# A fused retention and MLP kernel on one TensorE: first units reordered, part one's running sums on ScalarE and GpSimd, x^T copied in halves

## The chip, the core and the metric

The kernel runs on one core of one Trainium2 chip. A core has a matrix engine (TensorE, "PE" in the profile, with its weight loads as "PEld"), three engines for elementwise work (VectorE "DVE", ScalarE "ACT", GpSimd "POOL") and SyncE ("SP"), which here only issues transfers. The engines run side by side; each takes its own instructions in the order in which the program lists them, and semaphores hold an instruction back until its inputs are there. TensorE writes into accumulation banks (PSUM), from which VectorE or ScalarE copy the results into the core's memory.

The metric is the device time of one execution in microseconds (us).

## What is computed

```python
# q, k, v: (8, 8, 576, 64)  batch, heads, sequence, head size; float32
scores = scale * q @ k^T                       # per batch and head
ret = scores * Dmat                            # Dmat[i, j] = gamma[h] ** (i - j) for i >= j, else 0
attn = ret @ v
x = attn.transpose(0, 2, 1, 3).reshape(4608, 512)
h = x @ w_in                                   # w_in (512, 2048)
g = max(h, 0) + alpha * min(h, 0)              # alpha (2048,)
out = g @ w_out                                # w_out (2048, 512)
```

## The kernel before

**Retention in chunks.** The sequence of 576 rows is cut into nine chunks of 64. Within a chunk the scores are multiplied by a triangular mask; what earlier chunks contribute goes through a state of 64 x 64 per head, the running sum of k^T v over the chunks before. Powers of gamma are folded into q and v beforehand (`part_scale`, `scale_pair`).

**The MLP in units.** The 4608 rows of x are cut into 18 blocks of 256 (`kb`). The 2048 hidden columns are cut into eight groups (`i`) of two times 128. A *unit* is one (block, group): a first product (x^T with a slice of `w_in` into the bank `ph`), the activation on the engines beside TensorE (into `g`), and a second product (`g` with a slice of `w_out`, added up over the eight groups in the banks `po`). Blocks 2 to 17 use a form with seven instead of eight products and combined weights (`mlp_unit`, L450). Blocks 0 and 1, whose weights are only just arriving, use the plain form: `plain_unit` (L411), `plain_relu` (L430), `plain_out` (L391).

**Weights come in pieces.** Each group has four pieces: two for `w_in`, two for `w_out`, fetched as raw float64 words and turned into float32 on three engines. `piece_in` (L286) puts two ScalarE instructions into the program (L297, L299). `piece_out` (L302) puts in three on VectorE (L308, L311, L313) and one addition on GpSimd (L315), and then issues the next fetch. Pieces 0 and 1 are the first group's `w_in`, 2 and 3 its `w_out`, 4 and 5 the second group's `w_in`, 6 and 7 its `w_out`.

**The first batch in parts.** The retention of batch 0, from which blocks 0 and 1 are made, is computed ahead in three *parts* of 4, 4 and 1 chunks, all eight heads at once. The steps of a part `x`:

- `part_scale(x, i)` (L615): GpSimd multiplies q (`i` = 1) or v (`i` = 2) by its powers of gamma, two halves, L621.
- `part_transposes(x, i)` (L633): TensorE turns k or q, four tiles at a time, L641; copies at L648 (one of part zero's at L646).
- `part_scores(x)` (L650): TensorE L660, 64 instructions in the trace; mask at L667 (VectorE) for the first part, and at L669, L670 (copy on ScalarE, mask on GpSimd) for the second.
- `part_states(x)` (L672): TensorE L680, then the running sums: `sums[x][0..3]`. For the first part L688 copies on ScalarE the first bank slice, and L690 adds on VectorE one slice at a time.
- `part_values(x)` (L697): TensorE L706 with the masked scores, then L717 with the running sums; chunk `j` uses `sums[x][j - 1]`. Even chunks go into bank 0, odd ones into bank 1. Then x^T is copied out: L722 copies bank 0 (128 partitions x 512 elements), L724 copies bank 1 in two halves of 64 partitions.
- `part_carry(x)` (L693): GpSimd makes the start of the next part from the last sum, L694.

In the names "part one" of the change is part 0 of the code, and "q's part two" is q of part 1.

**Order.** Up to L881 the order of every engine's instructions is the order in which the program lists them (a manual schedule). L766 to L828 list the beginning by hand: parts, pieces and the units (0,0), (0,1), (1,0), (1,1) in turn. Then a loop (L864) does the other twelve plain units with the retention of two head pairs of batch 1 in the gaps, and after that the main loop runs the other blocks. A unit's second product is listed one unit after its first product.

**Loads.** SyncE issues nearly all loads in program order. In the beginning `load` (L78) holds a load back until the one that lies `IN_FLIGHT` = 5 x 256 KB of loads ahead of it has landed.

Of the kernel before, what the change touches and what calls it, by code (L numbers as in the profile page):

```python
# [14 lines left out]
ALU = mybir.AluOpType  # L15
# [3 lines left out]
def kernel(  # L19
# [10 lines left out]
    nc = tc.nc  # L30
# [5 lines left out]
    NPAIR = H // 2  # L36
# [32 lines left out]
    def half(x):  # L69
        return slice(x * C, (x + 1) * C)  # L70
# [1 line left out]

    IN_FLIGHT = 5 << 18
    flight = []

    def load(to, src, size):  # L78
        ins = nc.sync.dma_start(to, src)
        if gated[0]:  # L80
            ahead = size
            for other, n in reversed(flight):
                if ahead >= IN_FLIGHT:
                    tc.add_manual_dep(ins.ins, other.ins.name, mybir.DependencyInfo(
                        mybir.DependencyClass.Sync, mybir.DependencyReason.DATA),
                        reason="bytes in flight")
                    break
                ahead += n
            flight.append((ins, size))

    gated = [True]

# [59 lines left out]
    def load_part(x):  # L154
        j0, j1 = PARTS[x]
        for i, src in ((0, k), (1, q), (2, v)):
            for m in range((j1 - j0 + 1) // 2):
                s0 = (j0 + 2 * m) * C
                rows = min(P, j1 * C - s0)
                to, fro = part[x][i][0:rows, m], src[0, :, s0:s0 + rows].rearrange("h p d -> p h d")  # L160
                if x == 0 and i == 1:
                    nc.scalar.dma_start(to, fro)
                else:
                    load(to, fro, rows * DM * 4)
# [29 lines left out]
    for i in range(NBIT - 1):  # L194
# [8 lines left out]
                            op=ALU.mult)  # L203
# [61 lines left out]
    def fetch(n):  # L265
        while npiece[0] < min(n, len(pieces)):
            srcs, at = pieces[npiece[0]][0], npiece[0]
            npiece[0] += 1
            free[:] = [t for t in free if at < gone.get(t, len(pieces))]
            t = free.pop(0)  # L270
            if isinstance(t, str):
                raw = ring.tile([P, 4 * HM], INT32, tag=t, name=f"raw_{at}")
            else:
                raw = w_in[t][:, 4:6].rearrange("p s u c f -> p (s u c f)").bitcast(INT32)
            for i, src in enumerate(srcs):
                to = raw
                if len(srcs) > 1:
                    to = raw.rearrange("p (x e f two) -> p x e f two", x=2, e=2, two=2)[:, :, i]
                load(to, src, P * 4 * HM * 4 // len(srcs))
            raws.append((raw, t))  # L280
# [90 lines left out]
            t0 = kb * TB + m * P  # L371
            nc.sync.dma_start(out[t0:t0 + P, :], osb[:, m].rearrange("p x f -> p (x f)"))

    def mlp_out():
        kb, i, g = pend.pop(0)
        if kb in PLAIN:
            return plain_out(kb, i, g)
        if i == 0:
            acc[kb] = [ps_o.tile([P, 2, HM], FP32, tag=f"pso{n}", name=f"po{n}_{kb}")
                       for n in range(4)]  # L380
        for n, (x, y) in enumerate(PROD):
            nc.tensor.matmul(acc[kb][n // 2][:, n % 2, :], g[:, x, :], w_out[i][:, y, :],  # L382
                             start=(i == 0 and n % 2 == 0),
                             stop=(i == NU - 1 and (n % 2 == 1 or n == 6)),
                             skip_group_check=True)
        if i == NU - 1:
            out_block(kb, acc.pop(kb))

    def plain_out(kb, i, g):  # L391
        if i == 0:
            acc[kb] = [ps_o.tile([P, DM], FP32, tag=f"pso{2 * kb + m}", name=f"po{m}_{kb}")
                       for m in range(2)]
        for m in range(2):
            for x in range(2):
                nc.tensor.matmul(acc[kb][m], g[:, 2 * x + m],  # L397
                                 w_out[i][:, 2 * x:2 * x + 2].rearrange("p x f -> p (x f)"),
                                 start=(i == 0 and x == 0), stop=(i == NU - 1 and x == 1))
        if i == NU - 1:  # L400
            po = acc.pop(kb)
            osb = ring.tile([P, 2, DM], FP32, tag=f"o{kb}", name=f"osb_{kb}")
            for m in range(2):
                t0 = kb * TB + m * P
                nc.scalar.copy(osb[:, m], po[m])
                nc.sync.dma_start(out[t0:t0 + P, :], osb[:, m])
        if kb == PLAIN[-1] and i % UST == UST - 1:
            waiting.extend((w_in[i // UST], x) for x in S_WORK)
            waiting.extend((w_out[j], x) for j in range(i + 1 - UST, i + 1) for x in T_WORK)
# [262 lines left out]
    def part_states(x):  # L672
        kn, vn = part[x][0], part[x][2]
        banks = [t.rearrange("p (m c d) -> p m c d", m=2, c=NPAIR)
                 for t in part_banks(x, None if x == 0 else 0, "pu")]
        for m in range(2):
            for c in range(NPAIR):
                for p2 in range(2):
                    for h2 in range(2):
                        nc.tensor.matmul(banks[p2][half(h2), m, c], kn[half(p2), m, 2 * c + h2],  # L680
                                         vn[half(p2), m, 2 * c + h2],
                                         start=(m == 0 and c == 0),
                                         stop=(m == 1 and c == NPAIR - 1), skip_group_check=True)
        was = carry[x]
        for j in range(4):
            u = banks[j % 2][:, j // 2]
            if was is None:
                nc.scalar.copy(sums[x][j], u)  # L688
            else:
                nc.vector.tensor_tensor(out=sums[x][j], in0=was, in1=u, op=ALU.add)  # L690
            was = sums[x][j]
# [5 lines left out]
    def part_values(x):  # L697
        vn, qT, at = part[x][2], tT[x, 1], tat[x]
        banks = [t.rearrange("p (c m s) -> p c m s", c=NPAIR, m=2)
                 for t in part_banks(x, 0 if x == 0 else None, "pv")]  # L700
        for m in range(2):
            for c in range(NPAIR):
                for p2 in range(2):
                    for h2 in range(2):
                        n = 2 * c + m
                        nc.tensor.matmul(banks[p2][half(h2 ^ p2), c, m],  # L706
                                         vn[half(p2), m, 2 * c + h2],
                                         at[half(p2), h2, n * C:(n + 1) * C],
                                         start=(m == 0 and c == 0), stop=False,
                                         skip_group_check=True)  # L710
        for j in range(1 if x == 0 else 0, 4):
            su = sums[x][j - 1] if j else carry[x]
            for c in range(NPAIR):
                for h2 in range(2):
                    for e in range(0, D, 32):
                        to = (h2 ^ (j % 2)) * D + e
                        nc.tensor.matmul(banks[j % 2][to:to + 32, c, j // 2],  # L717
                                         su[half(h2), c, e:e + 32], qT[half(h2), c, chunk(j)],
                                         start=False, stop=(j >= 2), skip_group_check=True)
        xb[x] = ring.tile([P, NCC, TB], FP32, tag=f"x{x}", name=f"xb_{x}")  # L720
        to = xb[x].rearrange("p c (m q s) -> p q c m s", m=2, q=2)
        nc.scalar.copy(to[:, 0], banks[0])  # L722
        for h2 in range(2):
            nc.scalar.copy(to[half(h2), 1], banks[1][half(1 - h2)])  # L724


    def last_transposes():
# [37 lines left out]

    fetch(6)  # L766
    load_part(1)
    fetch(8)
    load_part(2)
    part_scale(0, 1)  # L770
# [1 line left out]
    part_transposes(0, 1)  # L772
    part_scale(0, 2)
    part_scores(0)
    part_states(0)
    piece_in(2)
    piece_out(2)
    part_carry(0)
    part_values(0)
    aps = ps_a.tile([P, NFC], FP32, tag="psa", name="aps")  # L780
    nc.tensor.transpose(aps, a16, ident[0:NFC, 0:NFC])
    nc.vector.tensor_copy(alpha, aps)
    nc.vector.tensor_scalar(nalpha, alpha, -1.0, None, ALU.mult)
    piece_in(3)
    piece_out(2)
    part_scale(1, 1)
    piece_in(1)
    plain_unit(0, 0)
    plain_relu()
    piece_out(1)  # L790
    part_scale(1, 2)
    part_transposes(1, 0)
    mlp_out()
    part_transposes(1, 1)
    piece_out(1)
    piece_in(1)
    piece_out(1)
    part_scores(1)
    part_states(1)
    part_scale(2, 1)  # L800
    part_scale(2, 2)
    piece_in(1)
    plain_unit(0, 1)
    piece_out(1)
    plain_relu()
    piece_in(1)
    part_values(1)
    part_carry(1)
    last_transposes()
    mlp_out()  # L810
# [14 lines left out]
    piece_in(1)  # L825
    piece_out(1)

    gated[0] = False  # L828

# [108 lines left out]
```

## Time and profile before

| | |
|---|---|
| median of the four runs | 1027.4 us (1026.47, 1027.32, 1027.48, 1028.34) |
| time of the profiled execution | 1027.32 us |
| its span, first to last instruction | 1025.6 us |
| TensorE: busy, share of the span | 1008.2 us, 98% |
| VectorE | 770.0 us, 75% |
| ScalarE | 267.4 us, 26% |
| GpSimd | 176.9 us, 17% |
| TensorE clock granted, mean | 0.996 |
| bytes moved | 64.30 MB, mean 63 GB/s |

The profiled execution is one of the four runs, 0.08 us from their median; 1.7 us of its time lie outside its span. TensorE's share is 6 tenths in the first of 40 slices (of 25.6 us each) and 9 tenths or more in all others but the last (8), and the granted clock is 8 tenths in the first slice and 9 or more after it. From 43.4 us on TensorE runs without a gap. Most of what the change touches lies in the first 45 us, so the table of the whole says little about it; that stretch is read from its timeline, its waits and its chain.

### The profile page before, as it was taken

The page shows a single profiled execution, that of the slowest core. Times are in us where ns is not written, and L with a number is a line of the kernel's source. Part 1 is how long each engine was busy: PE and PEld are TensorE (multiplying, and loading weights), DVE is VectorE, ACT ScalarE, POOL GpSimd, SP SyncE. Part 2 cuts the span into 40 slices and gives each one's busy share as a digit, 9 for nine tenths or more (in the row PEclk, how much of TensorE's full clock was granted, in tenths as well). Part 3 has the DMA queues.
Part 4 walks back from the last instruction along what each step waited for, and adds up shares of the span by engine and source line. Part 5 has one row for each costly group of instructions (what it writes and reads, how often), then busy time and mean ns, then how long its engine had stood idle before and what let it go on. Part 6 is the DMA issues. An engine that isn't in the chain of part 4 may idle for free.

```text
span 1025.6 us, 23101 instructions
## 1 busy us (share of the span) xinstructions
PE 1008.2 (98%) x9385; PEld 891.2 (87%) x9385; DVE 770.0 (75%) x2041; ACT 267.4 (26%) x599; POOL 176.9 (17%) x198
## 2 busy tenths in 40 slices
PE   6999999999999999999999999999999999999998
PEld 5666668999999999999999999999999999999997
DVE  7669967787877777776868787877788776667665
ACT  4556652223222222021122222222222211000000
POOL 4656675200200010100010000200020001010000
PEclk8999999999999999999999999999999999999999
DMA  9975744223223222112113222222222100000000
GB/s 237 232 196 141 184 74 102 42 62 60 61 43 67 49 42 61 24 45 43 40 34 68 45 53 45 65 44 61 48 47 57 24 22 2 22 1 21 1 21 22
DMA packets 229307, 64.30 MB, mean 63 GB/s; under 512 B 214336, under 2 KB 222544, under 8 KB 229200
## 3 DMA queue, kind: packets, MB, share of 16 engines
q1 hardware_dynamic: 227088, 62.29, 26.7%
q8 instruction: 74, 1.21, 0.5%
q10 hardware_dynamic: 2112, 0.53, 0.3%
q14 instruction: 33, 0.27, 0.1%
HBM read 53.35 MB, written 9.44 MB: 61 GB/s over the span
## 4 chain that ended last, share of the span: by engine, by line
PE 97%; DVE 1%; DMA 1%; issue 0%; ACT 0%; POOL 0%; SPq 0%; DVEq 0%; ACTq 0%
PE ph L462 40%; PE po L382 38%; PE po L397 6%; PE ph L418 5%; PE pv L600 3%; PE ps L551 2%; PE pu L570 2%; DMA w_out<-in_k_dram 1%; PE pt L641 0%; PE pv L717 0%; PE pv L706 0%; DVE w_out L690 0%; PE ps L660 0%; DVE wc L308 0%; DVE pa L667 0%
## 5 line engine op out<-in xcount | busy, mean ns | idle before, releaser
L382 PE MATMUL po<-w_out,g 128*128 128x256 f32 x1792 | 407.8, 380 | 0.0
L382 PEld LDWEIGHTS po<-w_out,g 128*128 128x128 f32 x1792 | 331.2, 191 | 39.3
L473 DVE TENSOR_TENSOR g<-ph,g 128x256 f32<-128x256 f32 (+1 forms) x512 | 187.8, 388 | 184.8 <-ACT g L468 112.6
L462 PE MATMUL ph<-xb,w_in 128*128 128x128 f32 x2048 | 277.8, 279 | 0.0
L462 PEld LDWEIGHTS ph<-xb,w_in 128*128 128x128 f32 x2048 | 253.2, 192 | 8.2 <-issue 0.5
L462 PE MATMUL ph<-xt,w_in 128*128 128x128 f32 x1536 | 213.4, 275 | 0.0
L462 PEld LDWEIGHTS ph<-xt,w_in 128*128 128x128 f32 x1536 | 192.2, 192 | 0.0
L468 ACT COPY g<-ph 128x128 f32<-128x128 f32 x128 | 33.9, 265 | 395.3 <-PE ph L462 373.3
L484 DVE TENSOR_TENSOR g<-g 128x128 f32<-128x128 f32 x512 | 126.8, 289 | 7.8
L478 DVE SCALAR_TENSOR_TENSOR g<-g 128x512 f32<-128x512 f32 x128 | 91.7, 716 | 3.9
L476 DVE TENSOR_SCALAR g<-g,alpha 128x256 f32<-128x256 f32 x256 | 84.9, 374 | 3.7
L523 POOL TENSOR_TENSOR qx<-qx,tabx 128x576 f32<-128x576 f32 x28 | 32.8, 1172 | 310.0 <-DMA qx<-in_q_dram 264.0
L418 PE MATMUL ph<-xb,w_in 128*128 128x256 f32 x256 | 60.6, 392 | 1.1 <-ACT xb L724 1.1
L559 DVE SCALAR_TENSOR_TENSOR mt<-ps,th,mask 64x320 f32<-64x320 f32 (+1 forms) x112 | 57.8, 516 | 4.5 <-PE ps L551 2.6
L397 PE MATMUL po<-w_out,g 128*128 128x512 f32 x128 | 58.5, 600 | 0.9 <-POOL w_out L621 0.9
L418 PEld LDWEIGHTS ph<-xb,w_in 128*128 128x128 f32 x256 | 49.4, 196 | 11.0 <-issue 3.6
L448 POOL TENSOR_TENSOR xt<-xb 128x256 f32<-128x256 f32 x16 | 11.6, 727 | 214.5 <-PE ph L462 202.3
L448 POOL TENSOR_TENSOR xt<-xb,xt 128x256 f32<-128x256 f32 x32 | 23.6, 737 | 143.0 <-ACT xb L609 142.3
L528 ACT ACTIVATE vn<-vn,tabv 64x576 f32<-64x576 f32 x56 | 43.3, 773 | 16.4 <-DMA vn<-in_v_dram 15.1
L397 PEld LDWEIGHTS po<-w_out,g 128*128 128x128 f32 x128 | 23.5, 190 | 24.9 <-issue 22.7
L589 ACT COPY vn<-su 64x512 f32<-64x512 f32 x56 | 34.5, 616 | 37.5 <-DVE su L583 36.8
L609 ACT COPY xb<-pv 128x256 f32<-128x256 f32 (+3 forms) x84 | 22.6, 321 | 79.1 <-PE pv L600 79.0
(120 smaller groups left out, 687.6 us busy)
## 6 DMA issues: line engine op xcount, KB each, us to landing
out_dram<-osb SPq DMA_DIRECT2D x36, 256.0 KB, 2.3
kx<-in_k_dram SPq DMA_DIRECT2D x112, 72.0 KB, 2.7
qx<-in_q_dram SPq DMA_DIRECT2D x112, 72.0 KB, 2.4
vn<-in_v_dram SPq DMA_DIRECT2D x56, 144.0 KB, 3.2
kn<-in_k_dram SPq DMA_DIRECT2D x56, 144.0 KB, 3.3
raw<-in_moe_w_in_dram SPq DMA_DIRECT2D x24, 256.0 KB, 4.7
raw<-in_moe_w_out_dram SPq DMA_DIRECT2D x10, 512.0 KB, 4.7
w_in<-in_moe_w_out_dram SPq DMA_DIRECT2D x6, 512.0 KB, 5.1
```

The costliest lines, as they stand in the source:

```text
L382: nc.tensor.matmul(acc[kb][n // 2][:, n % 2, :], g[:, x, :], w_out[i][:, y, :], start=(i == 0 and n % 2 == 0), stop=(i == NU - 1 and (n % ...
L397: nc.tensor.matmul(acc[kb][m], g[:, 2 * x + m], w_out[i][:, 2 * x:2 * x + 2].rearrange("p x f -> p (x f)"), start=(i == 0 and x == 0), sto ...
L418: nc.tensor.matmul(ph[:, x], w_in[i // UST][:, cc // 2 * 2 + x, i % UST, cc % 2], xb[kb][:, cc], start=(cc == 0 and x == 0), stop=(cc == N ...
L448: nc.gpsimd.tensor_tensor(out=o, in0=x0, in1=x1, op=ALU.subtract)
L462: nc.tensor.matmul(ph[m][:, o], w_in[i // UST][:, l, i % UST, cc], r[:, cc], start=(n in (0, 3) and cc == 0), stop=(n in (2, 6) and cc == ...
L473: nc.vector.tensor_tensor(out=o, in0=x0, in1=x1, op=ALU.add)
L476: nc.vector.tensor_scalar(g[:, 4 + 2 * m:6 + 2 * m], g[:, 2 * m:2 * m + 2], 0.0, alpha[:, fc:fc + 1], ALU.min, ALU.mult)
L478: nc.vector.scalar_tensor_tensor(out=g[:, 0:4].rearrange("p x t -> p (x t)"), in0=g[:, 0:4].rearrange("p x t -> p (x t)"), scalar=0.0, in1 ...
L484: ins = nc.vector.tensor_tensor(out=g[:, o, :], in0=g[:, x0, :], in1=g[:, x1, :], op=op)
L528: nc.scalar.activation(vn[x, h2], vn[x, h2], ACTF.Copy, scale=tabv[x, c:c + 1])
L559: nc.vector.scalar_tensor_tensor(out=mt[to, h2, p2::2], in0=ps[p2][half(x), 0:nm], scalar=th[to, 3, h:h + 1], in1=mask[to, None, :].to_bro ...
L589: nc.scalar.copy(vn[half(h2), h2, 1:], su[half(h2)])
```

## The change

It has six parts:

1. In `part_states(0)` ScalarE copies all four slices of the running sums out of the banks, and GpSimd adds them up in place; VectorE's three additions are gone. One `piece_in` is put between scores and states.
2. In `part_values(0)` x^T of block 0 is copied in two halves of its columns (`c`): three copies for the first two column groups, then three for the other two.
3. `plain_out` runs its four products in another order: the two row halves `m` inside, the weight half `x` outside; both banks are written in turn. Between the two values of `x` it calls a function if it is given one.
4. Unit (0,0)'s second product gets `part_transposes(1, 1)` as that function: q of the second part is turned in the middle of it, not after it.
5. The pieces of the first groups and the scalings of the last part are listed at other places: `piece_out` of piece 6 behind `part_scores(1)`, `part_scale(2, 1)` and `part_scale(2, 2)` behind the pieces 6 and 7.
6. The bytes in flight are raised from 5 to 7 x 256 KB once the second part's loads are listed.

SyncE's loads keep their order; some wait for a transfer one or two places earlier. On TensorE no instruction is added or removed.

```diff
-    IN_FLIGHT = 5 << 18
...
-        if gated[0]:
+        if in_flight[0]:
             ahead = size
             for other, n in reversed(flight):
-                if ahead >= IN_FLIGHT:
+                if ahead >= in_flight[0]:
...
-    gated = [True]
+    in_flight = [5 << 18]
...
-    def mlp_out():
+    def mlp_out(between=None):
         kb, i, g = pend.pop(0)
         if kb in PLAIN:
-            return plain_out(kb, i, g)
+            return plain_out(kb, i, g, between)
...
-        for m in range(2):
-            for x in range(2):
+        for x in range(2):
+            if x and between:
+                between()
+            for m in range(2):
                 nc.tensor.matmul(acc[kb][m], g[:, 2 * x + m],
...
         for j in range(4):
             u = banks[j % 2][:, j // 2]
-            if was is None:
+            if x == 0:
                 nc.scalar.copy(sums[x][j], u)
+                if j:
+                    nc.gpsimd.tensor_tensor(out=sums[x][j], in0=was, in1=sums[x][j], op=ALU.add)
             else:
                 nc.vector.tensor_tensor(out=sums[x][j], in0=was, in1=u, op=ALU.add)
...
-        nc.scalar.copy(to[:, 0], banks[0])
-        for h2 in range(2):
-            nc.scalar.copy(to[half(h2), 1], banks[1][half(1 - h2)])
+        for c in (slice(0, 2), slice(2, 4)) if x == 0 else (slice(0, NPAIR),):
+            nc.scalar.copy(to[:, 0, c], banks[0][:, c])
+            for h2 in range(2):
+                nc.scalar.copy(to[half(h2), 1, c], banks[1][half(1 - h2), c])
...
     load_part(1)
+    in_flight[0] = 7 << 18
     fetch(8)
...
     part_scores(0)
+    piece_in(1)
     part_states(0)
     piece_in(2)
     piece_out(2)
...
     nc.tensor.transpose(aps, a16, ident[0:NFC, 0:NFC])
+    piece_out(1)
     nc.vector.tensor_copy(alpha, aps)
     nc.vector.tensor_scalar(nalpha, alpha, -1.0, None, ALU.mult)
-    piece_in(3)
-    piece_out(2)
+    piece_in(2)
+    piece_out(1)
     part_scale(1, 1)
-    piece_in(1)
     plain_unit(0, 0)
     plain_relu()
     piece_out(1)
     part_scale(1, 2)
     part_transposes(1, 0)
-    mlp_out()
-    part_transposes(1, 1)
+    piece_in(1)
+    mlp_out(lambda: part_transposes(1, 1))
     piece_out(1)
     piece_in(1)
+    part_scores(1)
     piece_out(1)
-    part_scores(1)
     part_states(1)
-    part_scale(2, 1)
-    part_scale(2, 2)
     piece_in(1)
     plain_unit(0, 1)
     piece_out(1)
+    part_scale(2, 1)
     plain_relu()
     piece_in(1)
     part_values(1)
+    part_scale(2, 2)
     part_carry(1)
```

## The prediction, made before the changed kernel ran

> **What bounds the kernel now.** I read four views in this order: the chain that ended last over the whole span, the same chain over the first 70 us, the waits by engine there, and busy time and granted clock by stretch. The chain's shares by engine, then its pieces (start us, length us, what):
>
> ```profile
> PE 97%; DVE 1%; DMA 1%; issue 0%; ACT 0%; POOL 0%; SPq 0%; DVEq 0%; ACTq 0%
> ...
> 14.67 2.38 issue
> 17.05 1.08 PE pv L717 x52
> ...
> 18.15 0.58 ACT xb L722
> ...
> 19.35 0.59 ACT xb L724
> ...
> 20.07 5.74 PE ph L418 x16
> ...
> 27.58 3.67 PE po L397 x8
> 31.25 0.45 PE pt L641 x4
> ...
> 32.26 0.59 ACT w_out L648
> ...
> 38.28 1.24 POOL w_out L670
> ...
> 39.56 1.16 PE pv L706 x62
> ```
>
> TensorE sets the end: 97% of the chain is its own. What can be gained lies in the steps between its pieces, all before 43.4 us; an advance there moves all later work as a block. The same stops in the waits (engine and line, for what, total us, times, longest):
>
> ```profile
> PE pv L717 <- issue: 2.4, 1, 2.4
> PE ph L418 <- ACT xb L724: 1.1, 1, 1.1
> PE po L397 <- POOL w_out L621: 0.9, 1, 0.9
> PE pv L706 <- POOL w_out L670: 0.9, 1, 0.9
> PE ps L660 <- ACT w_out L648: 0.3, 1, 0.3
> ```
>
> The clock, by stretch (PE busy first, PEclk third from the right):
>
> ```profile
> 13.95:17.37 3.42, 1.04 (x73) 0.81 (x63) 3.19 (x6) 1.46 (x3) 0.79 (x1) 1.00 0.94 310
> 17.37:20.78 3.41, 2.27 (x76) 1.93 (x57) 2.59 (x5) 2.57 (x5) 2.35 (x3) 0.50 0.97 266
> 20.78:24.20 3.42, 3.42 (x10) 2.71 (x9) 3.21 (x5) 3.42 (x7) 1.27 (x1) 0.50 0.87 194
> ```
>
> In half-microsecond stretches the clock falls to 0.50 at 17.37 and is back at 24.20: 6.83 us, two equal stretches. TensorE was busy 30% of the one before the fall, 67% of the next (no return), 100% of the third (return). So unit (0,0)'s 16 instructions took 5.74 us; unit (1,0) at full clock takes 3.45.
>
> **Part by part.** Sums are made against the profiled execution, 1027.32 us.
>
> *x^T in halves.* Bank 0 is done at 18.13, bank 1 at 18.72 (L717: 17.05 + 1.67). Now L722 takes 0.58 and L724 twice 0.59, until 19.92; TensorE starts at 20.07. A copy of half the size is in the trace: L688, 128x256, 0.37, the next instruction 0.39 after it. So: bank 0's half 18.15 to 18.52, then bank 1, 18.75 + 0.39 + 0.37 = 19.51, start at 19.66: 0.41 earlier. The second half ends at 20.7; TensorE gets there after eight instructions, 21.9 at the earliest. If the clock still returns at 24.20, the 0.41 us hold one instruction more at 0.43, which saves 0.22 at the other end: **0.2 us**. If it returns at 20.78, 2.6 instructions are done by then and 13.4 follow at 0.216: the transposes start at 23.68, now 25.63: **1.95 us**. The trace has no such stretch: busy there rises from 2.27 to 2.68 of 3.41, 79%, between the rows 67% (stays) and 100% (returns), 36% of the way. The four runs spread over 1.9 us, so the stretches need not lie alike in each; I take 36% of the way: **0.8 us**, ends 0.2 and 1.95.
>
> *Sums on GpSimd.* Three L690 (0.42 each) leave VectorE; three copies of 0.39 on ScalarE and three additions (L694, same size, 0.61) are new. ScalarE now does a piece first: its bytes landed at 12 to 13 (SyncE issued its second half near 7.6, landing 4.2 to 5.8 later, and L297 ran at 13.05). The four copies then end at 14.8 to 15.8, the additions that L717 needs at 15.3 to 16.4. Cover: the 2.38 us stop at 14.67, which ends at 17.05. I read it as a wait for instructions: both TensorE rows show "issue", and queue 8 carries a block at 14.7. Without this cover L717 would need them at 15.15 (two of its thirds, 0.45 each at full clock, after 14.25) and wait 0.1 to 1.2 us. Behind the additions on GpSimd is piece 0's L315, then at 17.2 to 18.3, needed at 19.66. VectorE starts the pieces 0.6 to 1.2 earlier (14.31 now).
>
> *q turned inside the second product.* The copies L648 then run beside its second half, so the 0.29 us that L660 waits go: **0.3 us**. The turn waits for GpSimd's scaling of q (now 26.44 to 28.48, behind piece 3, which comes 1.8 earlier); TensorE gets there at 29.1, or at 27.4 with the early clock, the second landing of q being near 26.3. If q is late, half of the product waits behind it, up to 1 us in the early case. The 0.91 us before L397 stay: relu on ScalarE and VectorE, not moved.
>
> *GpSimd's order before values.* L670 now stands behind piece 6's L315 (35.76 to 37.06). With E for the end of unit (0,0) (25.81): v's scaling ends at E + 7.5, piece 5 at E + 8.75, L670 twice 1.25 then at E + 11.25; unit (0,1) ends at E + 12.1. The wait goes: 39.56 - 38.33, less two instructions already done, **1.2 us**. Late next: pieces 6 and 7 end at E + 13.9 (their product needs them at E + 15.9), and q's scaling of the last part, moved behind them, at E + 14.9, needed at E + 15.3. If that cover goes, 1.0 us a scaling.
>
> *Loads.* No order changes; piece 6 is issued some 0.3 us and piece 7 some 2.5 us earlier. Gain nothing: TensorE waits for no landing after 7.3. Loss: the DMA share is 0.9 to 1.2 already from 10 to 45 us, so 512 KB at 270 GB/s can push v by 1.9 us, from 28 to 29.9; its scaling starts at E + 5.5, 31.1. Covered; with the early clock 0.5 us would show.
>
> *Order of the second product, 16 units.* Same eight instructions, banks written in turn. The row: L382 changes bank every other product and has 0.0 us idle before it. Nothing. The Trainium skill (TensorE: Matmul & The Clock Gate, section "A second HAM failure mode: psum-queue depth-cycling") speaks against this: cycling through banks lets the array idle briefly and lose its clock again and again. By it the sum could turn to a loss; the clock in slices 2 to 40 of the page, over 0.9 with L382 running, does not show it.
>
> Sum: 0.8 + 0.3 + 1.2 = **2.3 us**, 1027.32 - 2.3 = 1025.0; ends 1.7 and 3.4, or 1025.6 and 1023.9. The median of the runs lies 0.08 from the profiled one, so it serves for both.
>
> **Rivals.**
>
> *The wait moves (no gain).* GpSimd or a landing takes the place of the waits removed: piece 6's landing stands ahead of the score copies on ScalarE (1.2), these ahead of L670. For it: in the trace GpSimd has no gap from 31.26 to 34.56 and from 35.76 to 42.7. Against it: 0.85 us of slack in the sum above, and piece 6 lands near 29.5 (24.4 + 5.0). The values follow a landing by 1.2 + 0.6 + 2.5; if it comes at 34.6, the 1.2 us are not gained and q's last scaling costs 0.5: 2.3 - 1.7 = 0.6, 1026.7.
>
> *A second stop for instructions (slower).* TensorE's 18770 instructions come in 74 blocks:
>
> ```profile
> q8 instruction: 74, 1.21, 0.5%
> ```
>
> 254 each, or 127 pairs of load and matmul. The second part's scores and states are 128 pairs in 2.05 us. In the trace the block for what follows is on its way at 30.8 and needed at 34.4. After the change TensorE's queue passes q's turn later relative to the scores: it enters the block before at 27.4, and the next is needed at 34.0 (32.3 with the early clock). My estimates of a fetch: the block of 30.8 was started 2.3 us after its request (the queue was free of q's scaling at 28.5); the first, asked for at 11 to 12 (half of the 222 pairs done by 14.67), came 5 to 6 us later, at 17.05. The rival decides if a fetch needs over 6.6 us (4.9 with the early clock). Price: as at 14.67, 2.38 us, and the low clock again, 5.74 - 3.45 = 2.29 for a unit and 0.5 for the short instructions: 5.2 - 2.3 = 2.9, 1030.2. The Trainium skill (Runtime: NRT & Kernel Launch, section "Instruction fetch mechanics") has such fetches as mostly hidden. The stop at 14.67 says they are not always; by the rule this rival costs nothing.
>
> *The product's order costs time.* 0.2 us for each of 16 units (L397 takes 3.43 or 3.63 us in the chain): 3.2 - 2.3 = +0.9, 1028.2; with 0.3 each, 1029.8. Against it: L382.
>
> **How the numbers follow.** Forecast, 0.62: 1025.0. The wait moves, 0.14: 1026.7. A second stop, 0.16: 1030.2. The order costs, 0.08: 1028.2 to 1029.8. About 0.2%, 2.05 us, is what can be told from no change; that is 1025.35. Of the forecast 0.55 lies below it and 0.07 above. Faster 0.55; same 0.07 + 0.14 + 0.04 = 0.25; slower 0.16 + 0.04 = 0.20. The forecast's own range is 1023.9 to 1025.6. For 8 in 10 it takes in the moved wait and, below, 0.6 us for stretches that lie better than the profiled ones: 1023.3 to 1028.3, which leaves out the second stop and the dearer half of the order's cost.
>
> **What will show it.** Right: L418 of unit (0,0) starts near 19.7; the scores follow q's turn and four product instructions without idle; no wait for GpSimd ahead of the second part's values; TensorE without gaps from 41.7 or earlier, now 43.4; L717's stop still near 14.7 to 17. The clock's return at 20.8 or at 24.2 decides between 3.4 and 1.7. Wrong: "issue" ahead of L680 or L418 after 30 us, a wait of q's or v's transposes and states for GpSimd, 8 instructions of the second product over 3.5 us, a wait for a landing after 43 us.

## The result, and the profile after

The changed kernel takes 1025.5 us (median of 33 runs, 1024.28 to 1028.05); the kernel before takes 1027.2 in the runs beside it. The ratio is 0.9987, its 95% interval 0.9982 to 0.9992. That is 1.3 us by the ratio and 1.7 by the medians; 2.3 were forecast, as 1025.0. The profiled execution took 1025.9 us, its span 1024.2: 1.4 less than before.

The chain that ended last in the changed kernel, from the parts of the first batch on (start us, length us, what):

```profile
14.87 0.35 PE pv L720 x14
15.22 2.24 issue
17.46 1.22 PE pv L720 x76
...
19.09 0.37 ACT xb L728
...
19.59 3.71 PE ph L419 x16
...
25.07 1.96 PE po L398 x4
27.02 0.87 PE pt L642 x8
27.89 1.72 PE po L398 x4
29.61 1.09 PE ps L661 x64
30.71 0.93 PE pu L681 x64
31.64 0.63 PE ph L419 x2
32.27 1.23 issue
33.50 3.29 PE ph L419 x14
36.79 1.09 PE pv L709 x64
37.88 0.72 PE pv L720 x44
38.61 1.09 issue
39.70 0.77 PE pv L720 x40
...
41.84 3.63 PE po L398 x8
```

q's turn (the 8 of L642) stands inside the second product, and the scores follow without idle time. No line of GpSimd is left in this stretch. But two pieces called "issue" are new: TensorE stops 1.23 us after two instructions of unit (0,1) and 1.09 us in the middle of the second part's values.

TensorE's waits over the first 70 us say the same (engine and line, for what, total us, times, longest):

```profile
PE pv L720 <- issue: 3.3, 2, 2.2
PE ph L419 <- issue: 1.2, 1, 1.2
PE po L398 <- DVE g L435: 0.8, 1, 0.8
PE ph L419 <- ACT xb L728: 0.8, 1, 0.8
```

Starts of the same steps in the timelines of TensorE, us (the chain's starts of L397/L398 in the last row):

| step | before | after | ahead by |
|---|---|---|---|
| unit (0,0), first product | 20.07 | 19.59 | 0.48 |
| k's turn, right behind it | 25.63 | 23.12 | 2.51 |
| second part's scores | 32.42 | 29.55 | 2.87 |
| unit (0,1), first product | 34.47 | 31.57 | 2.90 |
| second part's values | 38.33 | 36.72 | 1.61 |
| their second half (L717, L720) | 40.64 | 37.81 | 2.83 |
| x^T of the second part turned | 42.72 | 41.13 | 1.59 |
| unit (0,1), second product | 43.42 | 41.84 | 1.58 |

The table names the exchange. Of the 0.48 at the start of unit (0,0), 0.37 came from the copies (the wait ahead of the unit is 0.77 us, before 1.14; 0.41 were foreseen) and the rest from work ahead of them that ended 0.10 earlier. 2.03 came from unit (0,0) at full clock, 0.36 from the stretch with q's turn (0.29 of it is the scores' wait that is gone), 1.22 from GpSimd's wait that is gone: 4.1 us. The two stops took 1.29 and 1.24 back.

The clock did not fall in this execution: unit (0,0) took 3.71 us, before 5.74. That did not come from the copies: runs of this kernel with the same copies have the low clock too, as the next section shows.

### The profile page after: what moved, and what is told of

Its sections match the earlier page's. It is cut to its first block, busy times and chain, and to the rows that moved or that the text cites. A ratio compares the mean times of both kernels' runs of the same rounds, so it can differ in the third digit from the quotient of the medians.

```text
span 1024.2 us, 23109 instructions
## 1 busy us (share of the span) xinstructions
PE 1006.3 (98%) x9385; PEld 889.9 (87%) x9385; DVE 768.1 (75%) x2038; ACT 269.0 (26%) x605; POOL 179.0 (17%) x201
## 4 chain that ended last, share of the span: by engine, by line
PE 98%; DMA 1%; issue 1%; DVE 0%; ACT 0%; SPq 0%; DVEq 0%
PE ph L463 40%; PE po L381 38%; PE ph L419 6%; PE po L398 6%; PE pv L601 3%; PE ps L552 2%; PE pu L571 2%; DMA w_out<-in_k_dram 1%; PE pt L642 0%; PE pv L720 0%; PE ps L661 0%; PE pu L681 0%; PE pv L709 0%; DVE s L367 0%; PE pt L736 0%
## 5 line engine op out<-in xcount | busy, mean ns | idle before, releaser
L419 PE MATMUL ph<-xb,w_in 128*128 128x256 f32 x256 | 58.9, 383 | 2.0 <-issue 1.2
L398 PE MATMUL po<-w_out,g 128*128 128x512 f32 x128 | 58.6, 600 | 0.8 <-DVE g L435 0.8
L419 PEld LDWEIGHTS ph<-xb,w_in 128*128 128x128 f32 x256 | 47.9, 190 | 11.6 <-issue 4.0
L398 PEld LDWEIGHTS po<-w_out,g 128*128 128x128 f32 x128 | 23.4, 190 | 24.3 <-issue 21.7
```

Source lines behind the costliest of these rows:

```text
L398: nc.tensor.matmul(acc[kb][m], g[:, 2 * x + m], w_out[i][:, 2 * x:2 * x + 2].rearrange("p x f -> p (x f)"), start=(i == 0 and x == 0), sto ...
L419: nc.tensor.matmul(ph[:, x], w_in[i // UST][:, cc // 2 * 2 + x, i % UST, cc % 2], xb[kb][:, cc], start=(cc == 0 and x == 0), stop=(cc == N ...
```

## Is it the clock, and when? (the kernel after, once more)

Each run lists the mean granted clock of its core, also where it was not profiled. A stretch of 3.41 us at half clock lowers the mean by 0.0017. So 0.999 or more is no such stretch, 0.997 and 0.998 are about one (sometimes two, as rounding allows), 0.996 and less two or more. The start of the program is left out of this clock: in the nine profiles of kernels without the pad (below) TensorE took 1.55 or 1.99 us for the 64 pairs of the first scores, and 1.16 to 1.19 for those of the second part, but 1.00 is printed for both. So "full" here means from some 12 to 14 us on. The changed kernel ran unaltered a second time, beside other kernels.

> The changed kernel unaltered, on this chip beside the next two and for a second profile. Both theories: 1025.5, ratio 0.9982 to 0.9992. Theory, the block is a race between TensorE and a fetch of 2 to 5 us: if the clock falls in the profiled execution, TensorE is later and there is no stop at 475 pairs; if it does not fall, there is one of 0.5 to 1.5 us.

Measured: 1025.87 us, ratio 0.9991 (0.9982 to 1.0000). Its profile again had no fall of the clock and again both stops, 1.17 us after two of L419 and 1.09 after 50 of L720, at the same places in the program. The 45 runs of the changed kernel and the 94 of the kernel before that were made beside the experiments, sorted by their clock:

| mean clock | before: runs, median (range) | after: runs, median (range) |
|---|---|---|
| 0.999, 1.000 | 13, 1025.5 (1025.12 to 1025.77) | 11, 1025.1 (1024.25 to 1025.90) |
| 0.997, 0.998 | 33, 1026.5 (1025.77 to 1028.15) | 14, 1025.6 (1024.28 to 1028.13) |
| 0.996 or less | 48, 1027.4 (1026.85 to 1028.91) | 20, 1025.8 (1025.18 to 1028.93) |

In this table the change is worth 0.4 us with a full clock, 0.9 with about one low stretch and 1.6 with two or more. But 33 of its 45 runs were made in another set than the 94 (a set is what was run side by side on one chip). In the one set that lists the clocks of both kernels, that of this section, the three differences are 0.7, 0.6 and 0.6 us, from 3, 4 and 5 runs of the changed kernel. So the sorting shows that one and the same kernel is slower with the low clock (before by 1.9 us), and that the change gains in each group; that its gain depends on the clock is not shown.

Both profiles of the changed kernel kept the clock and have both stops. Of two relatives whose profiles have the low clock, the padded one (next section) has no later stop, and the one with 5 loads in flight has one of 0.50 us. This fits a race: TensorE that is late finds the blocks there. A profile of the changed kernel itself with a low clock does not exist.

## A stop for instructions, moved by 20 pairs

Theory: "issue" in these stops is a wait for a block of TensorE's instructions. Rival: a wait for something in the code at that place. The edit shifts the places by 20 pairs of load and matmul (in both kernels the same lines):

```diff
+    warm = ps_h.tile([P, 4 * P], FP32, tag="psh0", name="warm")
+    for n in range(20):
+        nc.tensor.transpose(warm[:, 0:P], ident, ident)
     load_part(1)
```

> The changed kernel with 20 extra transposes of the identity matrix at the start of TensorE's program, written to a bank that nobody reads; TensorE is idle there (the first k lands near 5 us), so they cost no time. Theory, instruction blocks: the three stops that the profile calls issue in the changed kernel stand after 222, 475 and 603 pairs of weight load and matmul, 253 and 128 apart, which is two blocks and one of 127. They are tied to the count, so each comes 20 of the kernel's own pairs earlier: the first after 58 of the 64 of L709 (now after 14 of L720), the second after 46 of the 64 of L681 (now after 2 of L419 in unit (0,1)), the third after 30 of L720 (now after 50). Rival, a wait for data that the profile does not name: the stops stay at their places in the program, after 14 of L720, 2 of L419 and 50 of L720.

Measured: 1025.5 us in one run. TensorE's waits in this run (columns as above):

```profile
PE pv L709 <- issue: 1.5, 1, 1.5
PE ph L419 <- POOL w_in L314: 1.4, 1, 1.4
```

The stop itself, in the timeline:

```profile
12.71 1.08 PE L709 MATMUL pv<-pa,w_out 64*64 64x64 f32 x57 [0.27 <-DVE pa L668]
15.27 0.34 PE L709 MATMUL pv<-pa,w_out 64*64 64x64 f32 x5 [1.48 <-issue]
```

The first stop had stood behind 14 of L720. It now stands behind 59 of L709's 64 (two stand ahead of the 57), which is 19 pairs earlier in the program: it goes with the count of instructions, not with the code. All four profiles with the pad have it there, and all nine without have it behind 14 of the values' second half. Counted from the first pair, the stops of the changed kernel lie at 222, 475 and 603: 253 and 128 apart, two blocks and one of 127 pairs. The rival is out for the first stop. The clock fell in this run (unit (0,0) took 6.37 us), and no later stop is there, so the places foreseen for the second and third were not seen.

The pad does a second thing, which the expectation left out. With it eight turns of k take 1.09 or 1.10 us in all four profiles, without it 1.97 (in the run without q's turn), and the 64 pairs of the first scores take twice 0.69 us, for 1.55 or 1.99. So TensorE runs at full pace earlier. The same kernel in more runs:

> The changed kernel with 20 more turned identity tiles at the start of TensorE's queue: the kernel of the first experiment, timed. Theory (the gain of the earlier work is partly taken back by stops for instruction blocks, which stand after a fixed count of pairs of load and matmul): the later block ends lie 20 pairs earlier in the program, at 455 and 583 pairs instead of 475 and 603; there the next block has been under way for longer before it is needed, and the two stops of 1.2 and 1.1 us shrink or go: 1024.0 to 1024.8 us, 0.7 to 1.5 below the changed kernel. Rival (the stops only move with the boundaries, or the 20 instructions cost what they save): 1025.5 us, no different from the changed kernel.

Measured: 1025.51 us, ratio 0.9989 (0.9980 to 0.9998): no faster than without the pad. The profile shows why. Its clock stayed full, and TensorE's waits from 20 to 60 us were these:

```profile
PE pt L642 <- DMA w_out<-in_k_dram: 1.4, 2, 1.0
PE pt L642 <- POOL w_out L622: 1.0, 1, 1.0
PE pt L736 <- POOL w_out L622: 0.8, 1, 0.8
PE pt L736 <- ACT xb L726: 0.7, 1, 0.7
```

Both later stops went, as the theory said. In their place TensorE waits for the landing of k's second part, for the scaling of q, for the copy of x^T and for the scaling of the last part. The second product of unit (0,1) starts at 41.11, only 0.73 earlier. Three limits lie within about 1 us of each other here: instruction blocks, GpSimd's order and landings.

## The parts of the change alone

**GpSimd's order ahead of the values**, put into the kernel before:

```diff
-    piece_out(1)
     part_scores(1)
+    piece_out(1)
     part_states(1)
-    part_scale(2, 1)
-    part_scale(2, 2)
     piece_in(1)
     plain_unit(0, 1)
     piece_out(1)
+    part_scale(2, 1)
     plain_relu()
     piece_in(1)
     part_values(1)
+    part_scale(2, 2)
```

> The kernel before, with only GpSimd's order of the second part changed as in the change: the pieces 6 and 7 behind the scores, the scaling of the last part behind them. The prediction's term: the 1.2 us that TensorE waited for the mask, ahead of the second part's values, go; ratio 0.9988. Theory, instruction blocks: the block after 603 pairs was on its way at 36.8 in the trace of before and would be there at 39.5; values that start at 38.3 instead of 39.56 need it at 40.0, so most of the 1.2 us stays gained, 0.8 to 1.2. Rival, the gain of this term was what the block took back: 0 to 0.3 us, ratio 0.9997 or more.

Measured: 1025.98 us beside 1027.23, ratio 0.9992 (0.9983 to 1.0001): 0.8 us, between 1.7 and -0.1, so nothing is just within it. All waits of TensorE behind 20 us in its profile (timeline: start us, us, what, idle before and its releaser):

```profile
25.54 3.67 PE L397 MATMUL po<-w_out,g 128*128 128x512 f32 x8 [1.16 <-DVE g L434]
...
30.38 1.18 PE L660 MATMUL ps<-w_out,w_out 64*64 64x64 f32 x64 [0.29 <-ACT w_out L648]
...
39.24 0.46 PE L732 MATMUL pt<-ident,w_out 64*128 64x64 f32 x4 [0.36 <-ACT xb L722]
39.91 0.46 PE L732 MATMUL pt<-ident,w_out 64*128 64x64 f32 x4 [0.21 <-POOL w_out L621]
```

The wait for L670 is gone and nothing of its size came in its place. This execution had the full clock and took 1024.29 us, as short as the shortest runs of the whole change.

**x^T in halves**, alone in the kernel before:

```diff
-        nc.scalar.copy(to[:, 0], banks[0])
-        for h2 in range(2):
-            nc.scalar.copy(to[half(h2), 1], banks[1][half(1 - h2)])
+        for c in (slice(0, 2), slice(2, 4)) if x == 0 else (slice(0, NPAIR),):
+            nc.scalar.copy(to[:, 0, c], banks[0][:, c])
+            for h2 in range(2):
+                nc.scalar.copy(to[half(h2), 1, c], banks[1][half(1 - h2), c])
```

> The kernel before, with only x^T of block 0 copied in halves. The prediction's term: 0.8 us, between 0.2 (clock back at the same stretch) and 1.95 (back one stretch earlier); ratio 0.9981 to 0.9998. Rival, from the trace of the changed kernel, in which the clock did not fall at all though the copies alone can't have done that: the clock's stretches lie differently in each execution and are no matter of the copies, so this is worth 0.4 us (the earlier start) or less, ratio 0.9996.

Measured: ratio 1.0000 (0.9992 to 1.0009). The wait ahead of unit (0,0) did shrink, 1.14 to 0.76 us. But TensorE then stopped for instructions in unit (0,1), without q's turn being moved (timeline):

```profile
33.15 0.48 PE L418 MATMUL ph<-xb,w_in 128*128 128x256 f32 x1
34.29 3.40 PE L418 MATMUL ph<-xb,w_in 128*128 128x256 f32 x15 [0.66 <-issue]
```

**Both together:**

> The kernel before with two parts of the change: GpSimd's order ahead of the second part's values, and x^T of block 0 copied in halves. Left out: the sums on ScalarE and GpSimd, q turned inside the second product, the order of the banks, the loads in flight. Theory (the order is worth most of the gain, the halves 0 to 0.2): 1025.6 to 1026.2 us, ratio 0.9986 to 0.9992. Rival (the parts add up as predicted, 1.2 + 0.8): 1025.2 us, ratio 0.998.

Measured: 1026.60 us, ratio 0.9996 (0.9987 to 1.0005). It is slower than both expectations; that the halves add to the order can't be seen. In the profile unit (0,0) waited for pieces 0 and 1 on GpSimd instead of the copies, 0.99 and 0.30 us, and the clock fell later, during the second product, which took 5.37 us for 3.67.

**All but q's turn** (the changed kernel with the turn behind the product again):

```diff
-    mlp_out(lambda: part_transposes(1, 1))
+    mlp_out()
+    part_transposes(1, 1)
```

> The changed kernel with q's turn of part two behind unit (0,0)'s second product again, not inside it. The prediction's term: the 0.29 us wait of the scores for ScalarE comes back, 0.3 us slower than the changed kernel, 1025.8. Rival, instruction blocks: TensorE's program passes q's turn earlier, and the scores come 0.3 us later, so the block of 475 pairs is in time and a stop of up to 1.2 us goes: 1024.6 to 1025.3, no slower than the changed kernel.

Measured: 1026.52 us, ratio 0.9996 (0.9984 to 1.0008): slower than both expectations, with an interval too wide to tell it from the changed kernel beside it (0.9991). In its profile, at full clock, no stop for instructions is left behind 20 us, but TensorE's waits over 10 to 60 us have these lines:

```profile
PE pv L709 <- POOL w_out L671: 1.3, 2, 0.9
PE pt L736 <- POOL w_out L622: 1.2, 1, 1.2
...
PE ps L661 <- ACT w_out L649: 0.3, 1, 0.3
```

The 0.3 us ahead of the scores are back, and TensorE, no longer held by instructions, waits 1.3 us for GpSimd's masks and 1.2 for the last part's scaling. This is the moved wait of the prediction's first rival, on the way it named: ScalarE idles 2.66 us for piece 6's landing, takes the piece up at 32.21, and only then copies the scores (33.35) that GpSimd's masks need. The prediction had the landing near 29.5; in the changed kernel ScalarE takes the piece up at 29.48, and the wait isn't seen there. The second product of unit (0,1) starts at 41.74, in the changed kernel at 41.77 by the same view: the one kernel loses to GpSimd what the other loses to the blocks.

**All but the loads in flight** (5 x 256 KB throughout, the line `in_flight[0] = 7 << 18` left out):

> The changed kernel with 5 instead of 7 x 256 KB of loads in flight. Theory, instruction blocks held up by loads: the blocks share the 16 transfer engines with the loads, and in the changed kernel the block needed at 475 pairs started 2 us later against TensorE than in e3; with fewer loads in flight it comes earlier, the stops shrink, 1024.5 to 1025.2. Rival, the depth of the loads does not matter to TensorE: as the changed kernel, 1025.5, within 0.3.

Measured: 1025.46 us, ratio 0.9982 (0.9973 to 0.9990); the changed kernel beside it had 0.9991 (0.9982 to 1.0000). The intervals overlap, so the depth can't be told from nothing. Its profile had one stretch at half clock and one later stop, 0.50 us.

**The same runs sorted by their clock.** Each value is the median of the kernel before less that of the kernel named, in us, within one set and one group of clocks, with the number of runs of the kernel named:

| kernel | 0.999, 1.000 | 0.997, 0.998 | 0.996 or less |
|---|---|---|---|
| before with the order alone | 1.0 (2) | 0.5 (7) | 0.7 (2) |
| before with halves alone | none | 0.5 (6) | 0.1 (5) |
| before with both | none | -0.2 (11) | none |
| after without the turn | 0.6 (2) | 0.35 (3) | 0.5 (6) |
| after with 5 in flight | 0.8 (2) | 1.5 (5) | 2.1 (4) |
| after | 0.7 (3) | 0.6 (4) | 0.6 (5) |

The order gains in each group. The 0.0 of the halves is partly a matter of the clock: none of their 11 runs kept it, but 4 of the 23 of the kernel before beside them. The groups are small, and how often the clock stays may itself depend on the kernel; so this is a sign, not a measurement.

## When a block is late

Queue 8 carries the instruction blocks. The start of the block that is needed at pair 475 was read from its traffic in stretches of 0.1 us, and set against the start of the second part's scores (negative: the block moves first):

| kernel, profile | block starts | against the scores | stop at 475 |
|---|---|---|---|
| before with order and halves | 29.4 | -3.1 | none |
| before with the order alone | 28.4 | -2.0 | none |
| after with 5 in flight | 29.1 | -1.9 | none |
| before | 30.8 | -1.6 | none |
| after without the turn | 28.0 | -1.1 | none |
| before with halves alone | 31.2 | +0.1 | 0.66 |
| after, second profile | 29.5 | +0.5 | 1.17 |
| after | 30.5 | +0.9 | 1.23 |

The three stops are the three cases where the block starts behind the scores. From the block's first bytes to the first instruction behind the stop 3.1, 3.4 and 3.0 us pass; scores and states last 2.05. What sets the block's start isn't settled: of the five profiles without the moved turn two have it at 30.8 and 31.2, three at 28.0 to 29.4.

## Spreading the short instructions (an own edit that lost)

Pairs of 64 x 64 run 128 in 2.05 us. The idea was to put long instructions between them: the states behind unit (0,1), the values' second half inside its second product, the last scores behind unit (1,0).

```diff
-    part_states(1)
...
     plain_unit(0, 1)
...
+    part_states(1)
...
-    part_values(1)
+    values = part_values(1)
+    next(values)
+    mlp_out(lambda: next(values, None))
...
+    last_scores()
     piece_in(1)
-    piece_out(2)
```

> The changed kernel with the short instructions of the second part spread out between long ones: the states (64 pairs) after unit (0,1)'s first product instead of before it, the 128 pairs with the running sums in the middle of unit (0,1)'s second product, the last part's scores after unit (1,0). No instruction is added or taken away. Theory, instruction blocks: TensorE stops because 128 short pairs (some 2 us) are used up before the next block has come (2.3 us from the start of its transfer, 4 to 6 from the request); with 16 or 8 long pairs of 3.5 us between, the stops of 1.23 and 1.09 us go: TensorE is without gaps some 2 to 3 us earlier, time 1022.8 to 1023.8 against 1025.5 for the changed kernel. Rival, data: the earlier work only meets the same waits, or those of the sums, masks and copies that now follow each other more closely: 1025 to 1026.5.

Measured: 1030.8 us, ratio 1.0038 (1.0025 to 1.0051), slower than before and than both expectations. One of the six executions, the profiled one, took 4437 us, 4.3 times as long as the others (1028.47 to 1032.72), so the same kernel was profiled again:

> The kernel of e2 once more, for its profile: the profiled execution of e2 ran at a sixth of TensorE's pace from end to end (4437 us) and shows nothing of its order, while its other five took 1028.5 to 1032.7. Theory, instruction blocks: no stop called issue at unit (0,1)'s first product or among the 128 pairs with the running sums; the 3 to 5 us that it lost then stand as named waits on ScalarE, VectorE or GpSimd, which the new order put behind each other. Rival, the blocks are late whatever the order: stops called issue of over 1 us at other places after 30 us.

Measured: 1029.27 us. TensorE's waits from 10 to 60 us:

```profile
PE ph L419 <- DVE w_out L749: 3.0, 1, 3.0
PE pv L721 <- issue: 2.9, 2, 2.1
```

There was no stop at 475, though in this run the clock fell, which may do that alone; the one at 603 was 0.75 us. It is still at pair 603, though that pair is now another instruction of the program (46 of L721, inside the second product): a second sign that the stops go with the count. But the mask of the last scores (L749) now stood on VectorE behind two pieces that ScalarE took up only at 46.55, behind its copies of x^T (from 42.58, when the moved values were done) and of the last part; and unit (1,1) waited 3.0 us for the bank that the mask frees. The edit lost to its own new wait, so it says nothing against the theory of blocks. The run shows one more thing: two stretches by the clock, cut at its fall (PE busy first, PEclk third from the right):

```profile
17.15:20.57 3.42, 2.71 (x61) 2.28 (x50) 2.51 (x6) 2.50 (x7) 2.72 (x3) 0.50 1.01 296
20.57:23.98 3.41, 3.41 (x9) 2.70 (x8) 2.08 (x3) 2.04 (x4) 1.16 (x2) 0.50 0.75 165
```

The first is busy for 2.71 of 3.42 us, 79%, the very case of the prediction, and the clock is not back behind it. With the halves alone, and with 5 loads in flight, the one low stretch was busy for this much, and the clock returned at its end:

```profile
18.80:22.21 3.41, 3.22 (x8) 2.59 (x9) 2.02 (x6) 3.34 (x8) 1.88 (x2) 0.50 0.81 193
19.10:22.51 3.41, 2.92 (x7) 2.41 (x8) 2.41 (x6) 3.34 (x8) 2.08 (x3) 0.50 0.94 222
```

That is 94% and 86%. In these profiles the bound lies between 79% and 86%.

## The pad in the kernel before

> The kernel before with the 20 turned identity tiles alone. Theory: it has only the first stop for instructions (2.38 us), and the 20 pairs move that one to an earlier place, where it was 1.5 us in the first experiment: 0 to 0.8 us below the kernel before, and the distance to the padded changed kernel is larger than that between the two unpadded ones (over 1.7 us). Rival (the pad is worth the same in both, or nothing): the distance stays 1.3 to 1.7 us.

Measured: 1025.14 us, ratio 0.9988 (0.9980 to 0.9997): both expectations missed. The pad alone gives the kernel before as much as the whole change gives. In its profile the first stop is the cheaper one, 0.94 us for 2.38 (over all profiles: 0.94 to 1.48 in the four with the pad, 1.45 to 2.38 in the nine without), and L670's wait is still there:

```profile
PE pv L706 <- issue: 0.9, 1, 0.9
...
PE pv L706 <- POOL w_out L670: 0.9, 1, 0.9
```

That is not a matter of more runs with a kept clock: sorted as above, the pad is worth 0.9 us (2 runs), 1.2 (8) and 1.0 (1).

Why the same pad gave the changed kernel nothing can be read from the timelines of ScalarE, which copies x^T out. The change puts three pieces ahead of these copies, before there were two. All in us:

| | changed | changed with pad | before with pad |
|---|---|---|---|
| values end (L720, L717) | 18.67 | 16.89 | 16.64 |
| third piece on ScalarE starts | 16.03 | 16.00 | behind the copies |
| copies of x^T start | 18.30 | 17.17 | 16.27 |
| unit (0,0) starts | 19.59 | 18.41 | 18.18 |

Without the pad the first stop covers the third piece. With it the values are done earlier, but ScalarE is still at the piece, whose landing it had awaited for 0.72 us: the copies start 0.28 behind the end of the values, not 0.37 ahead of it. So the padded changed kernel starts unit (0,0) later than the padded kernel before, in spite of the halves.

So the order was added to the padded kernel before:

> The kernel before with the 20 turned identity tiles and GpSimd's order ahead of the second part's values, nothing else of the change. Theory: in the padded kernel before, the wait of 0.9 us for the score masks is still there and no later stop for instructions is; the order takes that wait away, and the block ends at 455 and 583 pairs stop nothing: 1024.2 to 1024.6 us, 0.5 to 0.9 below the padded kernel before (1025.14), and about 1 us below the changed kernel. Rival (limits lie close behind one another: the scaling of q, its landing or an instruction block stops TensorE instead): 1025.0 to 1025.5 us, no better than either.

Measured: 1024.75 us (1023.89 to 1026.49), ratio 0.9983 (0.9974 to 0.9992), between the two expectations. In its profile the clock was low for two stretches, unit (0,0) took 5.57 us, no later stop and no wait for L670 was there, and the second product of unit (0,1) started at 40.75, 1.02 earlier than in the changed kernel at full clock (41.77 by the same view). It has the lowest median of all kernels here, with 20 extra pairs and three moved lines; but its interval overlaps that of the changed kernel, so that it is faster than it is likely, not shown.

## Why the prediction was right, point by point

- **What bounds the kernel: right.** TensorE's advance at 41.8 us (1.58) is close to that of the span (1.4).
- **GpSimd's order, 1.2 us: right in mechanism.** The wait for L670 (1.22 us at the values' second half) is gone in every profile that has the order in the kernel before, or together with the turn. Alone it gives 0.8 us, between -0.1 and 1.7: the largest of the parts tried alone, but not clear of nothing.
- **x^T in halves, 0.8 us: mis-sized, the step that failed.** The 0.41 us at the copies were nearly right: the wait ahead of unit (0,0) went from 1.14 us to 0.77, and to 0.76 with the halves alone. The weight of 36% for an early return of the clock was wrong: 79% busy does not bring it back. Nor do the copies decide whether the clock falls: the 3.41 us ahead of each fall (eight profiles) were busy for 30 to 57%, and in the kernel before the fall at 17.37 comes ahead of the first copy, 18.15. Even the 0.2 that then remain are not seen at the end: alone the halves gave 0.0, between -0.9 and 0.8, and in the profiles the next limit (a block, piece 0) stands where they would have gained.
- **q's turn, 0.3 us: right at its place** (scores without idle before them; 0.29 back in the run without the turn), not resolved in the time.
- **Sums at nothing: held.** The first stop still stood at pair 222 and still covered them: the additions ran from 14.57 to 16.92 (15.3 to 16.4 were foreseen for their end), the stop ended at 17.46. With the stop ended at 15.27 by the pad the values still ran without a wait for the sums. What the stop also covered, and the prediction reckoned only against the sums, is the piece more on ScalarE ahead of the copies: with the pad unit (0,0) waits 1.38 and 1.37 us, for 0.77. The profile of the first padded run names piece L314 for it, but the addition of piece 0 had ended at 17.2, and the copies of x^T ended at 18.32, 0.15 ahead of the unit's start, the same distance as without the pad.
- **Loads at nothing, product's order at nothing: held.** L398 still takes 3.63 and 3.43 us for eight. The depth of the loads alone was not resolved in the time.
- **The second stop for instructions, held for 0.16 likely: it came, in part.** It was in both profiles of the changed kernel, at the place named (unit (0,1) and the second part) and by the mechanism named; "issue" ahead of that unit's first product after 30 us was one of the prediction's own signs of being wrong. Its price was too high: not one stop of 2.4 us with a low clock behind it, but two of 1.2 and 1.1 with the clock kept.

That the total was near is in part luck: two errors nearly cancel. In the execution that was profiled the work came 4.1 us earlier, not 2.3, since the clock stayed; 2.5 went to the stops. In the median of many runs the change pays 1.3 to 1.7. That is under the 2.05 us that the prediction took as the line for "faster" (0.55): the gain is clear of nothing, but it lies in what the prediction called "same" (0.25).

## What to carry to other kernels

When the engine that bounds the kernel runs ahead, ask what feeds it besides data: its own instructions come in blocks, and many short ones in a row can use a block up before the next is there. Where several limits lie within a microsecond, removing one is worth only the distance to the next, so add the parts up on one time line and not as a sum. And sort the runs by the granted clock, beside runs of the same set, before the gain of an edit is read from them: the halves' 0.0 became 0.5 and 0.1.

## What the runs showed of the chip

- A wait for a block of TensorE's instructions held it up for 0.5 to 2.4 us. At pair 475 it came in the three of eight profiles in which the block began to move behind the start of the 128 short pairs, and 3.0 to 3.4 us passed from its first bytes to the first instruction run. The Trainium skill (Runtime: NRT & Kernel Launch, "Instruction fetch mechanics") calls the crossing of a block "mostly hidden". Its size agrees (256 there; 18770 instructions in 74 blocks are 254 here); hidden it is not in this kernel's first 45 us.
- The same program had a full mean clock (0.999 or 1.000) in 13 of 94 runs and not in the others. The Trainium skill (TensorE: Matmul & The Clock Gate, "Part 1: The HAM clock gate") has the clock judged by windows of 3413 ns that run on regardless of the kernel's start. The stretches here, 3.41 us each and beginning at 15.6 to 19.1 in the profiles where the clock fell before unit (0,0)'s end, agree with that.
- Twenty pairs that compute nothing made the kernel before 1.2 us faster by the ratio (interval 0.3 to 2.1). The cheaper first stop and the early full pace of TensorE both stand in the padded profiles; which of them is the cause was not tested.
